# Three reorderings in a Fourier-mixing and MLP kernel: bank copies and gelus, two builds and an output, the queues of the final stores

## The chip, the cores and the metric

The kernel runs on one core of one Trainium2 chip. A core has five engines that work through their own instruction streams and meet at semaphores: TensorE (PE in the profile, its weight loads PEld), VectorE (DVE), ScalarE (ACT), GpSimd (POOL) and SyncE (SP). SP, ScalarE and GpSimd can issue DMAs. TensorE writes its sums into eight banks of PSUM, each 128 partitions by 512 fp32 values.

The metric is the device time of one execution in microseconds. Before the change it is 861.91 us, the median of three runs (861.89 to 861.96).

## The reference

With x of 2048 rows and 640 columns (fp32), the kernel computes a layer norm without parameters, and adds a Fourier mixing of the result and a two-layer MLP of the result to x:

```python
xn = _layernorm(x)                                   # over the 640 columns
a = einsum("bsd,ed->bse", xn, dft_hid_re)            # DFT along the columns
b = einsum("bsd,ed->bse", xn, dft_hid_im)
y = einsum("ts,bse->bte", dft_seq_re, a) - einsum("ts,bse->bte", dft_seq_im, b)   # along the rows
h = gelu(xn @ w1 + b1)                               # 1536 hidden columns
out = x + y + h @ w2 + b2
```

## The kernel before, in words

All products are fp32 products made of three matmuls (`product`, L274, its matmuls at L277, L278 and L279; `hidden`, L289, at L301): each operand is split into a rounded high part and the rest (`split`, L154: ScalarE makes the high part at L160, VectorE the rest at L161), and high by high, high by low and low by high are summed in one bank. The order of all work is written out by hand: what stands first in the code is first on its engine's queue, and an instruction that waits holds whatever stands behind it on the same engine. The rows are worked on in four blocks of 512.

The first stage is the MLP. Blocks 0 and 1 go through it in the plain way: for each of twelve units of 128 hidden columns, `hidden` (TensorE), `gelu` (ScalarE) and `output` (TensorE, five banks). Meanwhile the layer norm of the later blocks runs.

Blocks 2 and 3 go through the first MLP layer together, in six pairs of units, q = 0 to 5, by a scheme with seven instead of eight products for a two by two block. Each pair has three parts on TensorE: `head(q)` (L799), `mid(q)` (L843) and `finish(q)` (L856). A pair uses five banks, called y, d, x2, z2 and w_. `head` computes into y, ScalarE copies y to x2 (`copy_bank`, L796, with its instruction at L797), `head` goes on into d, and ScalarE copies d to SBUF as `fifth` (L804). `mid` adds a product to y, ScalarE copies y to z2, and TensorE goes on with products into x2 and then into z2; after that VectorE adds `fifth` to y and writes the sum of z2 and `fifth` to w_. `finish` adds the last products to z2, y and w_. `head(q + 1)` stands between `mid(q)` and `finish(q)`, and takes over banks that pair q - 1 has used.

`act(q, blk, k)` (L837) is one gelu on ScalarE: it reads a finished bank of pair q for block 2 (blk 0) or block 3 (blk 1) and parks the result in SBUF. In the loop over q (L1080 to L1110) the gelus of the pair behind, p = q - 1, are issued beside the products of pair q. Where p is even, both gelus of block 2 belong to the loop's start; where p is odd, the first of them was issued in `mid(p)`. `sums_w1` (VectorE), `split_w1` (ScalarE, VectorE; its tile is tw) and `load_rq` (SP) prepare the weights of the next pairs, and `between` is what `mid` calls behind its copy to z2. `prep_w` prepares weights of the Fourier stage (ScalarE and VectorE into wst, in the profile wstp; then GpSimd stores them as wit, L394).

After the pairs comes the second MLP layer, one unit after the other: block 2 for n = 0 to 11 into banks 0 to 4 and then block 3 for n = 12 to 23 into banks 5, 6, 7, 3 and 4. At n = 12 block 3 takes two units together: 18 matmuls into banks 5 to 7, and then those into banks 3 and 4, which block 2 has used. `beside_second(n)` (L1135) is what the other engines do behind unit n: `split_h` (the split of two parked gelu results; its tiles are hs and xtt), the weights of later units, `outs(2, ...)` (L864) at n = 11, and the builds. `outs` puts block 2's five banks out: for each, ScalarE adds the bias in the bank (L344), VectorE transposes it into one of two buffers ot (L347), and GpSimd adds it to x (L349), in the order of banks 3, 4, 0, 1, 2; SP stores the result as ys and later starts the loads of raw.

`build(k, what)` (L561) makes operands of the Fourier stage from the rows of the normed input: k is 0 to 7, xr its loaded rows (`load_xr`, SP, L558), and `what` names the parts made: "ab" (tile xab) or "c" (tile xc). Builds 0 to 3 are also stored to DRAM by GpSimd (`formed`, L1125). Builds 4 and 6 are made in two steps, "ab" first and "c" later.

Then comes the Fourier stage, over 500 us of the span, with the same kind of products on halves of the rows; its last steps store the results. `store` (L1236) issues four DMAs, one for each group of 32 partitions, to rows that lie 16 to a partition; each store's pieces in DRAM are as long as the columns stored, 128 bytes for a chunk of 32 columns. The last block's odd chunk (columns 128 to 160 of each group, `yb4`, tile y) is stored just before the end, and the last two chunks of the other block (k = 2 and 3, tile yo, L1674 to L1681) when TensorE has ended or nearly so: chunk 2 needs a transpose and an add, chunk 3 a transpose alone (L1678) of the very last bank. All stores go by SP unless `on_act` gives the last few of the four to ScalarE's queue; the store before them (`out_b`, tile u) goes by ScalarE's queue as a whole.

Of the kernel before, what the change touches and what calls it, by code (L numbers as in the profile page):

```python
# [16 lines left out]
Q = 4  # L17
B = 32
# [8 lines left out]
def kernel(  # L27
# [38 lines left out]
    nc = tc.nc  # L66
# [11 lines left out]
    DQ = D // Q  # L78
# [576 lines left out]
    for tag, size, keys in PLACES:  # L655
        t = whole[tag] = place(tag, (P, size // 4))
# [13 lines left out]
    last = 1  # L670
# [119 lines left out]
    for _ in range(5):  # L790
        y, d, x2, z2, w_ = PB[-1]
# [45 lines left out]
    def act(q, blk, k):  # L837
        y, d, x2, z2, w_ = PB[q]
        src = ((x2, y), (z2, w_))[blk][k]
        u = 2 * q + k  # L840
        nc.scalar.activation(park(q, blk, k), bank(src), AF.Gelu_apprx_tanh, bias=b1c[:, u : u + 1])
# [148 lines left out]
    for g in range(NG):  # L990
        t, i = divmod(g, NF)
# [87 lines left out]
    late_steps = {1: (6, 7), 2: (8, 9), 3: (10, 11), 4: (12, 13)}  # L1079
    for q in range(1, NF // 2):  # L1080
        p = q - 1
        if not p % 2:
            act(p, 0, 0)
        sums_w1(q + 1)
        act(p, 0, 1)

        def between():
            split_w1(q + 1)
            load_rq(q + 2)
            act(p, 1, 0)  # L1090
            act(p, 1, 1)

        mid(q, between)
        if q < NF // 2 - 1:
            head(q + 1)
        else:
            second(2, 0, 0, HU[0, 0])
            split_h(1)
            for u in (2, 3):
                split_w2(u)  # L1100
                raw_w2(u + 4, u - 2)
        for k in late_steps.get(q, ()):
            prep_w(k)
        finish(q)
        if q == 3:
            split_h(0)
        if q == 4:
            prep_w(14)
            for u in range(2, 6):
                raw_w2(u, u - 2)  # L1110
# [24 lines left out]
    def beside_second(n):  # L1135

        if n % 2 and 2 <= (n + 3) // 2 < NF:
            split_h((n + 3) // 2)
        for u in {1: (4, 5), 2: (6,), 3: (7,), 4: (8,), 5: (9,), 6: (10,)}.get(n, ()):
            late_w2(u)  # L1140
        if n == 6:
            load_xo(2)
        if n in (2, 4, 6, 8):
            formed(n // 2 - 1)
            load_xr((2, 3, 4, 6)[n // 2 - 1])
        if n == 9:
            build(4, "ab")
        if n == 11:
            outs(2, (3, 4, 0, 1, 2))
            A["es"].close()  # L1150
            A["raw"] = pool("rawp")
            load_a(0)
        if n == 12:
            build(6, "ab")
        if n == 13:
            load_a(1)
        if n == 14:
            A["xcp", 0] = place("xc01", (P, 2, 2, 7 * P))
            build(4, "c")
        if n == 16:  # L1160
            build(5)
        if n == 17:
            load_xr(7)
            build(6, "c")
        if n == 19:
            build(7, "a")
        if n == 21:
            A["r01"] = place("r01", (P, 2, 2, 2, TB), F32)
            turn(0, 0)
            turn(0, 1)  # L1170
            A["as"] = place("as", (P, 3, 2, 2, TB))
        if n == 22:
            form(0)
            turn(1, 0)
            turn(1, 1)
            form(1)
        if n == 23:
            form(2)
# [54 lines left out]
            for k in names:  # L1233
                nc.sync.dma_start(part_of(t, k), sums[t, k])

    def store(t, src, c0, c1, on_act=0):  # L1236

        for q in range(Q):
            (nc.scalar if q >= Q - on_act else nc.sync).dma_start(
                rows_of(out, t)[:, :, q * DQ + c0 : q * DQ + c1], src[q * B : (q + 1) * B]  # L1240
            )

# [42 lines left out]
    yo = {}  # L1285
# [183 lines left out]
    def hidden_beside(b, n):  # L1469


        ta, tb = blocks[b - 1][1], blocks[b][1]
        last = b == len(blocks) - 1
        x_, y_, z_ = (banks[:, k : k + 2] for k in (X, Y, Z))
        us, vs = bank(US), bank(VS)
        ya = yo[ta]

        def s(which, k):
            return sums[(ta, tb)[which], k]

        def t2(k):
            return lambda: add(s(1, KU[k]), s(1, KV[k]), s(1, KU[k]), ALU.subtract)

        def t3(k):
            return lambda: add(s(0, KU[k]), s(1, KU[k]), s(0, KU[k]), ALU.subtract)

        def t4(k):
            return lambda: add(s(0, KV[k]), s(0, KV[k]), s(1, KU[k]), ALU.subtract)

        def columns(k):  # L1490

            return s(1 if last else 0, ("u1", "u2")[k]).rearrange("p a b -> p (a b)").rearrange("p (n e) -> p n e", n=NB)

        def load_yb(k):
            return lambda: nc.sync.dma_start(columns(k), ys[k][tb])

        def copy(dst, src):
            return lambda: nc.scalar.activation(dst, src, AF.Copy)

        def to(dst, acc, name, then=lambda: None):  # L1500


            def f():
                add_turned(dst, turned(acc, name))
                then()

            return f

        def out_a(c0, c1):
            return lambda: store(ta, ya[:, :, c0:c1], c0, c1) if last else None  # L1510

        def odd():
            yt = turned(us, f"yo_{tb}")
            add_turned(ya[:, :, 4 * B :], yt)
            add_turned(yo[tb, 4], yt)
            out_a(4 * B, DQ)()

        def in_two(k):

            acc, name = s(1, ("v2", "v1")[k]), f"yb{k}_{tb}"  # L1520

            def f():
                if name not in A:
                    A[name] = turned(acc, name)
                else:
                    add_turned(columns(k), A.pop(name))
                    out_b(k)()

            return f

        def out_b(k):
            return lambda: store(tb, columns(k), 2 * k * B, 2 * (k + 1) * B, Q if last and k == 1 else 0)

        def last_columns():

            A["end"] = A["rt2"][:, 0, 0, 0]
            nc.vector.transpose(A["end"].rearrange("p (n i) -> p n i", i=B), ya[:, :, 3 * B : 4 * B])

        yb1, yb2 = in_two(0), in_two(1)
        yb4 = to(yo[tb, 4], vs, f"yb4_{tb}", lambda: store(tb, yo[tb, 4], 4 * B, DQ))  # L1540
        f5s = [lambda u=u: f5(u) for u in range(2)] if not last else [lambda: None] * 2
        f6s = [lambda u=u: f6(u) for u in range(2)] if not last else [lambda: None] * 2
        v1 = lambda: add(s(1, "v1"), s(1, "v1"), x_)
        end = lambda: add(bank(X + 1), bank(X + 1), A["end"])
        pre = [v1] if n == 17 and not last else []
        post = {

            0: [lambda: gather(1, tb, "v1", z_), lambda: gather(1, tb, "v", vs, op=ALU.subtract), f5s[0]],
            1: [f5s[1]],
            3: [to(ya[:, :, : 2 * B], x_, f"ya1_{ta}")],  # L1550
            2: [last_columns] if last else [],
            4: [t2(0)],
            5: [t2(1)],
            6: [to(ya[:, :, : 2 * B], y_, f"ya2_{ta}", out_a(0, 2 * B)), t2(2)],
            7: [odd],
            8: [t3(0)],
            9: [copy(s(1, "v1"), z_), t3(1)],
            10: [t3(2)],
            11: [t4(0)],
            12: [copy(s(1, "v2"), x_), t4(1)],  # L1560
            13: [load_yb(0), t4(2), load_yb(1)] if last else [t4(2)],
            14: [lambda: add(s(1, "v2"), s(1, "v2"), z_), yb1],
            15: [yb1] if last else [load_yb(0)],
            16: [] if last else [load_yb(1)],
            17: [v1, end, yb2, yb2] if last else [yb1, yb2],
            18: [yb4] if last else [yb2],
            19: [f6s[0]],
            20: [] if last else [f6s[1], yb4],
        }.get(n, [])
        if not last:  # L1570
            if n in (12, 13):
                post.insert(0, lambda: load_g(b, (NW - 1) * ND + 13 - n))
            if n == 18:
                post[:0] = [lambda k=k: load_part(blocks[b + 1][1], k) for k in ("u1", "u")]
            if n == 20:
                post.append(lambda: load_a(put_off[0]))

                def end():
                    to(ya[:, :, 2 * B : 4 * B], x_, f"ya3_{ta}")()
                    store(ta, ya, 0, DQ)  # L1580

                later.append(end)
        return pre, post
# [88 lines left out]


    t = blocks[-2][1]  # L1674
    for k, on_act in ((2, Q), (3, Q // 2)):
        d = yo[t][:, :, k * B : (k + 1) * B]
        if k == 3:
            nc.vector.transpose(d, bank(X + 1).rearrange("p (n i) -> p n i", i=B))  # L1678
        else:
            add_turned(d, turned(bank(X), f"yt_{k}"))  # L1680
        store(t, d, k * B, (k + 1) * B, on_act)  # L1681


# [29 lines left out]
```

## Time and profile before

| what | us |
|---|---|
| median of three runs | 861.91 |
| profiled execution, its own time | 858.26 |
| its span, first to last instruction | 856.5 |
| TensorE busy | 843.5 |
| VectorE busy | 661.5 |
| ScalarE busy | 353.7 |
| GpSimd busy | 45.5 |

The profile is one execution, and its time stands 3.65 us below the median of the runs. The granted clock of TensorE was 0.998 over the span. The page of the profile gives busy times and the costliest groups of instructions. The waits list who waited for whom, with the total, the number and the longest. The chain of waits follows the work that ended last back to the start. The timeline lists instructions in order of time: start and duration in us, engine, line, operation, what it writes and reads, the count where several are merged, and in brackets how long its engine had been idle before and what ended that. A `q` behind an engine's name (SPq, ACTq) is its queue of DMA issues. For a DMA, "landing" is the time from its issue to its completion.

### The profile page before, as it was taken

What the parts mean: (1) busy time and instruction counts of PE and PEld (TensorE: products, weight loads), DVE (VectorE), ACT (ScalarE), POOL (GpSimd) and SP (SyncE); (2) the same over time, 40 slices, a digit from 0 to 9 for tenths busy, and PEclk for the clock granted to TensorE, in tenths of its full rate; (3) what the DMA queues carried; (4) which work ended last, traced back from release to release, by engine and by line L of the source; (5) the groups of instructions that cost most, each with busy time, mean ns of one, the idle gap of its engine ahead of it and who ended that gap; (6) DMA issues with size and microseconds to landing.
All of it is one profiled execution on the core that took longest, in us unless ns stands there. A gap on an engine that the chain in (4) does not pass through costs nothing.

```text
span 856.5 us, 10320 instructions
## 1 busy us (share of the span) xinstructions
PE 843.5 (98%) x3711; PEld 695.7 (81%) x3711; DVE 661.5 (77%) x831; ACT 353.7 (41%) x495; POOL 45.5 (5%) x65
## 2 busy tenths in 40 slices
PE   7999999999999999999999999999999999999997
PEld 6888888878878788888888888888888888888885
DVE  6644756786657788889988787998977998885686
ACT  6443634456656544334434334232322423222241
POOL 0000211031211120000000000000000000000000
PEclk9999999999999999999999999999999999999999
DMA  6657698937669998938843769753765779704464
GB/s 185 201 153 200 141 226 240 216 82 189 203 210 341 356 209 156 205 86 199 183 136 86 184 194 302 167 136 98 205 172 168 253 183 233 304 19 178 124 180 96
DMA packets 209219, 158.45 MB, mean 185 GB/s; under 512 B 82896, under 2 KB 182736, under 8 KB 208656
## 3 DMA queue, kind: packets, MB, share of 16 engines
q1 hardware_dynamic: 199936, 136.16, 62.3%
q0 software_dynamic: 3952, 20.71, 6.0%
q10 hardware_dynamic: 5280, 0.92, 0.6%
q8 instruction: 29, 0.48, 0.2%
q14 instruction: 22, 0.18, 0.1%
HBM read 114.76 MB, written 42.99 MB: 184 GB/s over the span
## 4 chain that ended last, share of the span: by engine, by line
PE 84%; issue 7%; DMA 4%; POOL 2%; DVE 2%; ACT 1%; SPq 1%; POOLq 0%; DVEq 0%; ACTq 0%
PE banks L277 25%; PE banks L278 25%; PE banks L279 25%; PE banks L301 10%; DMA xr<-xs 1%; POOL wit L394 1%; DMA wz<-in_A_dft_hid_im_dram 1%; DMA x<-in_A_x_dram 1%; DMA forms_c<-xcst 1%; POOL xo L349 1%; DMA ys<-xo 0%; SPq L364 0%; PE banks L667 0%; DMA rq<-in_B_w_dram 0%; DVE xtt L161 0%
## 5 line engine op out<-in xcount | busy, mean ns | idle before, releaser
L279 PE MATMUL banks<-as,xab 128*128 128x512 f32 x411 | 159.9, 389 | 0.0
L277 PE MATMUL banks<-as,xab 128*128 128x512 f32 x411 | 159.9, 389 | 0.0
L278 PE MATMUL banks<-as,xab 128*128 128x512 f32 x411 | 159.9, 389 | 0.0
L160 ACT ACTIVATE as<-r 128x1024 fp32r<-128x1024 f32 x80 | 85.0, 1062 | 175.8 <-PE banks L279 155.5
L161 DVE TENSOR_TENSOR as<-r,as 128x1024 fp32r<-128x1024 f32 x80 | 97.1, 1215 | 41.7 <-ACT as L160 41.7
L277 PEld LDWEIGHTS banks<-as,xab 128*128 128x128 f32 x411 | 77.1, 188 | 16.1
L278 PEld LDWEIGHTS banks<-as,xab 128*128 128x128 f32 x411 | 77.1, 188 | 16.0
L279 PEld LDWEIGHTS banks<-as,xab 128*128 128x128 f32 x411 | 77.1, 188 | 15.9
L277 PE MATMUL banks<-as,xc 128*128 128x512 f32 x224 | 87.1, 389 | 0.0
L278 PE MATMUL banks<-as,xc 128*128 128x512 f32 x224 | 87.1, 389 | 0.0
L279 PE MATMUL banks<-as,xc 128*128 128x512 f32 x224 | 87.1, 389 | 0.0
L160 ACT ACTIVATE as<-rt 128x1024 fp32r<-128x1024 f32 x32 | 34.0, 1063 | 70.5 <-PE banks L279 62.5
L301 PE MATMUL banks<-xtt,xab 128*128 128x512 f32 x240 | 56.7, 390 | 0.0
L301 PEld LDWEIGHTS banks<-xtt,xab 128*128 128x128 f32 x240 | 44.9, 188 | 9.5 <-DVE xtt L161 0.2
L277 PEld LDWEIGHTS banks<-as,xc 128*128 128x128 f32 x224 | 42.0, 188 | 8.8
L278 PEld LDWEIGHTS banks<-as,xc 128*128 128x128 f32 x224 | 42.0, 188 | 8.7
L279 PEld LDWEIGHTS banks<-as,xc 128*128 128x128 f32 x224 | 42.0, 188 | 8.7
L161 DVE TENSOR_TENSOR as<-rt,as 128x1024 fp32r<-128x1024 f32 x32 | 38.7, 1211 | 5.3 <-ACT as L160 5.3
L320 DVE TENSOR_TENSOR hs<-ab,hs 128x512 fp32r<-128x512 f32 x24 | 17.6, 732 | 32.1 <-ACT hs L318 32.1
L160 ACT ACTIVATE as<-u 128x1024 fp32r<-128x1024 f32 (+1 forms) x24 | 22.1, 919 | 48.2 <-PE banks L279 48.2
L488 DVE STREAM_TRANSPOSE r<-raw 128x1024 f32<-128x1024 f32 x32 | 39.5, 1239 | 0.9 <-PE banks L279 0.3
L488 DVE STREAM_TRANSPOSE rt<-raw 128x1024 f32<-128x1024 f32 x32 | 38.8, 1230 | 0.9 <-PE banks L279 0.8
(335 smaller groups left out, 1615.3 us busy)
## 6 DMA issues: line engine op xcount, KB each, us to landing
raw<-in_A_dft_seq_re_dram SPq DMA_DIRECT2D x64, 256.0 KB, 5.4
raw<-in_A_dft_seq_im_dram SPq DMA_DIRECT2D x64, 256.0 KB, 5.2
ws<-wit SPq DMA_DIRECT2D x15, 384.0 KB, 5.2
x<-in_A_x_dram SPq DMA_DIRECT2D x16, 320.0 KB, 4.6
xs<-x SPq DMA_DIRECT2D x64, 80.0 KB, 1.8
xo<-in_A_x_dram SPq DMA_DIRECT2D x16, 320.0 KB, 6.4
xab<-wit SPq DMA_DIRECT2D x13, 384.0 KB, 4.1
wit<-wstp POOLq DMA_DIRECT2D x12, 384.0 KB, 4.4
```

The source lines that it names most:

```text
L160: nc.scalar.activation(h, s, AF.Copy)
L161: nc.vector.tensor_tensor(l, s, h.bitcast(F32), op=ALU.subtract)
L277: nc.tensor.matmul(acc, wh, mh, start=first, stop=False, skip_group_check=goes_on)
L278: nc.tensor.matmul(acc, wh, ml, start=False, stop=False, skip_group_check=goes_on)
L279: nc.tensor.matmul(acc, wl, mh, start=False, stop=last, skip_group_check=goes_on)
L301: nc.tensor.matmul(acc, W1[i][:, a, j * P : (j + 1) * P], XT[j][:, b], start=n == 0, stop=n == len(steps) - 1)
L320: nc.vector.tensor_tensor(hs[:, 1], a, hs[:, 0].bitcast(F32), op=ALU.subtract)
L349: eng.tensor_tensor(d, d, yt.rearrange("p (n i) -> p n i", i=B), op=ALU.add)
L394: nc.gpsimd.dma_start(wits[w][j], t[:, :, :n].bitcast(F32))
L488: nc.vector.transpose(held(pieces[g][2], u).rearrange("p c (n i) -> p c n i", i=B), r.rearrange("p n (c i) -> p c n i", i=B))
```

## The change

There are three edits.

First, in the loop over the pairs the gelus of block 2 of the pair behind move from ahead of `mid(q)` into `between`, so that on ScalarE they come behind the copy of y to z2 and ahead of `split_w1`. `sums_w1` stays where it was.

Second, "ab" of build 4 moves from n = 9 to n = 12 and "ab" of build 6 from n = 12 to n = 13 in `beside_second`. On ScalarE and VectorE they thereby come behind the split of n = 11 and `outs(2, ...)`, and build 6 behind the split of n = 13.

Third, `store` takes a list of queues. The odd chunk's four stores of the last block go by GpSimd's queue instead of SP's. Chunks 2 and 3 of the end alternate between SP and ScalarE; before, chunk 2 went by ScalarE alone and chunk 3 half by SP, half by ScalarE.

```diff
     for q in range(1, NF // 2):
         p = q - 1
-        if not p % 2:
-            act(p, 0, 0)
         sums_w1(q + 1)
-        act(p, 0, 1)
 
         def between():
+            if not p % 2:
+                act(p, 0, 0)
+            act(p, 0, 1)
             split_w1(q + 1)
             load_rq(q + 2)
             act(p, 1, 0)
...
-        if n == 9:
-            build(4, "ab")
         if n == 11:
             outs(2, (3, 4, 0, 1, 2))
...
         if n == 12:
+            build(4, "ab")
+        if n == 13:
             build(6, "ab")
-        if n == 13:
             load_a(1)
...
-    def store(t, src, c0, c1, on_act=0):
+    def store(t, src, c0, c1, on_act=0, queues=None):
 
         for q in range(Q):
-            (nc.scalar if q >= Q - on_act else nc.sync).dma_start(
+            (queues[q] if queues else nc.scalar if q >= Q - on_act else nc.sync).dma_start(
...
-        yb4 = to(yo[tb, 4], vs, f"yb4_{tb}", lambda: store(tb, yo[tb, 4], 4 * B, DQ))
+        yb4 = to(
+            yo[tb, 4], vs, f"yb4_{tb}", lambda: store(tb, yo[tb, 4], 4 * B, DQ, queues=[nc.gpsimd] * Q if last else None)
+        )
...
-    for k, on_act in ((2, Q), (3, Q // 2)):
+    for k, queues in ((2, [nc.sync, nc.scalar] * 2), (3, [nc.sync, nc.scalar] * 2)):
...
-        store(t, d, k * B, (k + 1) * B, on_act)
+        store(t, d, k * B, (k + 1) * B, queues=queues)
```

## The prediction

> **What bounds the kernel now.** I read the page first, then the waits of TensorE, then the chain of waits, and last the timelines of the engines around each wait of the chain.
>
> ```profile
> span 856.5 us, 10320 instructions
> PE 843.5 (98%) x3711; PEld 695.7 (81%) x3711; DVE 661.5 (77%) x831; ACT 353.7 (41%) x495; POOL 45.5 (5%) x65
> ```
>
> TensorE is busy for 98% of the span, and no edit changes a matmul. Time can only come from its idle places and from what lies behind its last matmul. Its waits are few (columns: total, times, longest, us):
>
> ```profile
> PE banks L667 <- DVE xp L208: 2.4, 1, 2.4
> PE banks L648 <- DVE warm L639: 1.9, 1, 1.9
> PE banks L277 <- DVE ot L347: 1.5, 1, 1.5
> PE banks L277 <- ACT banks L797: 1.0, 1, 1.0
> ```
>
> The first two are the start, which the edits leave alone. The other two, L347 (outs) and L797 (copy_bank), are what the first two edits move. The chain of waits shows the larger one in order of time, and the end (start, duration, what):
>
> ```profile
> 283.06 12.02 DMA xr<-xs
> 295.10 1.14 ACT xab L582 x3
> 296.24 0.96 ACT xtt L160
> 297.22 1.23 DVE xtt L161
> 298.45 0.64 DVE ot L347
> 299.13 0.50 PE banks L277
> 299.63 0.23 PE banks L278
> ...
> 850.04 0.24 PE banks L279
> 850.30 0.72 DVE yo L1678
> ```
>
> A load of 12.02 us holds the fifth build on ScalarE (xab), the split queued behind it follows, then the transpose that frees the bank, then TensorE. In flow a matmul starts 0.23 us after the last one, while its row lasts 0.39 us; a wait counted from the modelled end is therefore 0.16 us short of the time lost. Behind the last matmul (850.28) the span runs another 6.2 us.
>
> ```profile
> 246.36 0.50 PE L277 MATMUL banks<-xtt,tw 128*128 128x512 f32 x1 [1.04 <-ACT banks L797]
> ```
>
> ```profile
> 299.13 0.50 PE L277 MATMUL banks<-hs,xc01w 128*128 128x512 f32 x1 [1.46 <-DVE ot L347]
> ```
>
> **Edit 1: copies ahead of gelus.** Five bank copies pass eight gelus on ScalarE (two where the pair behind is even, one where it is odd). Nothing is added, and no DMA or VectorE instruction moves against its own queue.
>
> ```profile
> 193.89 0.58 ACT L797 ACTIVATE banks<-banks 128x512 f32<-128x512 f32 x1
> 194.38 1.05 ACT L160 ACTIVATE tw<-rq 128x1024 fp32r<-128x1024 f32 x1
> 198.71 0.58 ACT L797 ACTIVATE banks<-banks 128x512 f32<-128x512 f32 x1 [1.54 <-PE banks L279]
> ...
> 244.57 1.25 ACT L841 ACTIVATE pa<-banks,b1c 128x512 f32<-128x512 f32 x2
> 245.71 0.60 ACT L797 ACTIVATE banks<-banks 128x512 f32<-128x512 f32 x1
> 246.22 1.26 ACT L841 ACTIVATE pb<-banks,b1c 128x512 f32<-128x512 f32 x2
> ```
>
> In the last pair the copy starts at 245.71 behind two gelus and TensorE starts when it ends (246.31 + 0.05 = 246.36). In front it starts at 244.57, where the gelus did: 1.14 us earlier. TensorE would then start at 245.22; its last matmul before was 0.39 + 1.04 us ahead of 246.36, at 244.93, and in flow the next is due at 245.16. So 0.06 us of the wait stays and **1.14 us** is gained. The gelus end as before (the pb row still begins at 246.22), so the banks of pair 4 come free as before or, for the first two, 0.5 us later, at 246.35; the first matmul that writes one of them is due after six more matmuls, 245.22 + 1.4 = 246.6.
>
> In the other pairs TensorE does not wait for this copy, so I cost them at nothing, and the cover must be named. In pairs 1 and 3 the copy itself waits for TensorE, and the two gelus now fall between it and the tw split, which goes back by their 1.14 us: from 194.38 to 195.52, its end to 196.6.
>
> ```profile
> 195.47 1.23 DVE L161 TENSOR_TENSOR tw<-rq,tw 128x1024 fp32r<-128x1024 f32 x1 [3.66 <-ACT tw L160]
> 196.61 1.38 DVE L428 TENSOR_TENSOR banks<-banks,fifth 128x512 f32<-128x512 f32 x2
> ```
>
> VectorE then ends tw at 197.87 and the two bank sums at about 199.1. The next head's product with tw begins when its six matmuls before it end (the copy at 198.71 waits for them): 198.45. Cover 0.6 us. finish's product over the second bank begins six matmuls later, 199.81: cover 0.7 us. Both are thin. If they were gone, each microsecond beyond them would be lost at two places; none is, by these rows. Pairs 2 and 4 keep their tw split, which waits for VectorE's sums of weights. Queued behind the split is SP's load of rq, needed a whole pair (12 us) later.
>
> **Edit 2: builds five and seven follow block 2's outputs.** Four ScalarE and five VectorE instructions of build 4 go behind the split of n = 11 and outs, and those of build 6 behind the split of n = 13. No DMA is moved: ys stores and raw loads stay behind outs on SP, and earlier outs lets them go earlier.
>
> ```profile
> 289.80 1.05 ACT L160 ACTIVATE hs<-pb 128x1024 fp32r<-128x1024 f32 x1
> 297.10 2.94 ACT L344 ACTIVATE banks<-banks,b2c 128x512 f32<-128x512 f32 x5
> ```
>
> On the clock of before: the split follows hs on ScalarE at 290.8, done on VectorE (1.23 us, behind hs there) by about 293.4. TensorE lost 1.46 + 0.16 = 1.62 us, so without the wait its matmul would come at 297.51; 18 matmuls stand before it (4.08 us), so block 2's last unit is issued by 293.43. Two biases of 0.59 us (2.94/5) and two transposes of 0.64 us end near 294.9. That is 2.6 us before 297.51, so the wait goes entirely: **1.62 us**. What is late next: VectorE stands in outs for POOL.
>
> ```profile
> 299.21 6.49 POOL L349 TENSOR_TENSOR xo<-xo,ot 128x512 f32<-128x512 f32 x5 [7.63 <-DVE ot L347]
> ```
>
> Five adds at 1.3 us with two buffers hold the last transpose until near 298, and build 4's sums start behind it. Before, build 4 stood for its load until 295.10, and outs behind it waited for the same POOL adds until they neared their end at 305.7, with build 6 behind them. So build 6 and the splits behind it end earlier, not later. I cost that at nothing.
>
> **Edit 3: the end.** The odd chunk's four stores leave SP for GpSimd, and the eight last ones alternate between SP and ScalarE (four each; before two and six).
>
> ```profile
> 849.22 0.95 ACTq L1239 DMA_DIRECT2D out_dram<-yo  x2
> 851.57 1.50 ACTq L1239 DMA_DIRECT2D out_dram<-yo  x3
> ```
>
> ```profile
> 847.67 2.08 SPq L1239 DMA_DIRECT2D out_dram<-y  x4
> 851.05 0.85 SPq L1239 DMA_DIRECT2D out_dram<-yo  x2
> ```
>
> ScalarE issues two, stands from 850.17 to 851.57, then issues four, the last at 853.11:
>
> ```profile
> L1239 ACTq DMA_DIRECT2D out_dram<-yo x1: 499/499/499, 853.1 to 853.1; - x1
> DMA to landing us min/median/max: 2.1/2.1/2.1
> ```
>
> It lands at 855.2, and 1.3 us later the span ends. The stand fits a completion semaphore that the odd chunk's second store held (issued 848.03, lands after 3.5 us):
>
> ```profile
> L1239 SPq DMA_DIRECT2D out_dram<-y x1: 573/573/573, 848.0 to 848.0; - x1
> DMA to landing us min/median/max: 3.5/3.5/3.5
> ```
>
> In the changed program's order the last ScalarE store waits for the first chunk-2 store on SP in this way. That one is issued at 849.22 and lands 2.1 to 3.5 us later (the two rows just shown), 851.3 to 852.7; the last store is then issued at 851.5 to 852.7 and lands at 853.6 to 855.2. Gain 0 to 1.6 us; I take the middle, **0.8 us**, since the rows of three queues still overlap.
>
> GpSimd's price for a store of 512 runs of 128 B isn't in the trace. The nearest rows are its weight stores, of 128 runs (three column groups together) or 256 (two):
>
> ```profile
> L394 POOL DMA_DIRECT2D wit<-wstp x21: 539/558/951, 203.0 to 245.4; - x21
> DMA to landing us min/median/max: 2.4/4.2/5.5
> ```
>
> Flat, four cost 4 x 0.56 = 2.2 us, the last issued at 849.3, landing by 849.3 + 4.2 = 853.5, under the end above. In proportion to runs from the longest row (0.95 us at 256), 1.9 us each: issued to 855.3, landing near 857.7, 2.5 us after 855.2. I take the flat value, as 128 and 256 runs give nearly the same, and keep 2.5 us of loss as the other end.
>
> The rows of the engines at the end (span, then PE, PEld, DVE, ACT, POOL, clock, DMA share, GB/s):
>
> ```profile
> 851.00:852.00 1.00, 0.00 (x0) 0.00 (x0) 0.02 (x1) 0.00 (x0) 0.00 (x0) 1.00 0.81 96
> 853.00:854.00 1.00, 0.00 (x0) 0.00 (x0) 0.00 (x0) 0.00 (x0) 0.00 (x0) 0.55 1.07 166
> ```
>
> They are less loaded while ScalarE stands than after, so an earlier issue has room. [...]
>
> **The sum.** 1.14 + 1.62 + 0.8 = 3.56 us against the profiled execution's own 858.26 (span 856.5): 854.7. The runs shown have a median of 861.91, 3.65 us above it; I take the gain over unchanged: **858.4 us**.
>
> **The rivals.** About 0.2% (1.7 us) is what a measurement of this kernel can tell from no change.
> - *Slower: GpSimd's stores end last.* With t us per store, issued one behind the other from 847.67 and landing 2.4 us after the last, the end is 847.67 + 4t + 2.4. It passes 855.2 at t = 1.3, eats TensorE's gain of 2.76 at t = 2.0, and from t = 2.4 the kernel is slower by over 0.2%; at t = 2.6 the end is 860.5, 5.3 us later than before, and the time 861.91 - 2.76 + 5.3 = 864.4. For it: two to four times the runs of the rows, and a GpSimd that issued nothing for 500 us. Against: 128 and 256 runs at 0.54 to 0.95 us, which puts 512 at 1.9 at most. Chance 0.06. The milder half, t = 1.5 to 2.4, gives 860.0 to 863.6: chance 0.09.
> - *One wait comes back elsewhere.* A cover of 0.6 us fails in pairs 1 and 3, or the transposes wait for something not seen here. Of the 2.76 us some 1.2 to 1.6 stay, with the tail's 0.8 in all 2.0 to 2.4: 859.5 to 859.9. For it: the thin covers. Against: they are the same rows in a new order. Chance 0.10.
> - *The tail gains nothing.* The engines and not the issue set the end: the same bytes have to land, and a landing of 3.5 us beside 2.1 us shows them queueing. 861.91 - 2.76 = 859.2. Chance 0.15.
> - *No change.* The waits of the profiled execution are not in the runs shown, which take 3.65 us longer for a reason the profile can't show: 861.9. Chance 0.05.
>
> **How the numbers follow.** The forecast has 0.55, with its own range 857.6 (tail 1.6) to 858.9 (tail 0.3). The range goes from 857.4 to 860.9, into the milder GpSimd case; outside lie no change, the slower rival and half of the milder one, 0.16. Faster: 0.55 + 0.15 + 0.10 + 0.02 of the milder case = 0.82; same: 0.05 + 0.07 = 0.12; slower 0.06.
>
> **What would show it.** Edit 1: the L797 row gone from TensorE's waits, the pair's copy ahead of pa, tw split of pair 1 about 1.2 us later and no new wait for tw or for bank sums. Edit 2: the L347 row gone, ot transposes beside the last matmuls of block 2, the xr load out of the chain. TensorE's last matmul near 847.5. Edit 3: chunk stores on both queues without the stand of 1.4 us, the last landing some 4.1 instead of 4.9 us after the last matmul, POOL's four rows of about 0.6 us. The prediction is wrong if POOL's rows are over 1.3 us each or land last, or if a new row of over 0.5 us stands among TensorE's waits.

## The result, and the profile after

| | before | changed |
|---|---|---|
| median of 8 runs each, side by side, us | 859.73 (856.63 to 861.96) | 854.82 (853.63 to 855.13) |
| ratio, 95% interval | | 0.9943 (0.9921 to 0.9964) |
| profiled execution: its own time, span | 858.26, 856.5 | 854.27, 852.5 |
| start of the first transposes (L667), us | 11.09 | 9.69 |
| start of the last matmul | 849.88 | 846.07 |
| last landing | 855.21 | 851.18 |

The change is faster by 4.9 us in the medians, where 3.5 us was predicted, and its time is 3.6 us below the predicted 858.4. The kernel before has a median of 859.73 here, not the 861.91 of the three runs that the prediction started from (they are among the eight). A second difference turned out to be the key: the kernel before scatters by 5 us over these runs, the changed one by 1.5.

The page after, first two lines, which answer to those shown of before:

```profile
span 852.5 us, 10322 instructions
PE 844.2 (99%) x3711; PEld 696.2 (82%) x3711; DVE 660.9 (78%) x831; ACT 354.2 (42%) x495; POOL 48.2 (6%) x69
```

TensorE's waits after (total, times, longest, us):

```profile
PE banks L648 <- DVE warm L639: 1.9, 1, 1.9
PE banks L667 <- DVE xp L208: 0.3, 1, 0.3
```

The rows of L347 (1.5) and L797 (1.0) are gone, as edits 1 and 2 were to do. The row of L667 is the start: 2.4 us before, 0.3 here. No edit touches the start; the loads of x simply landed earlier in this execution (the slowest of the first four took 4.3 us to land, 6.0 us before). In the profiles below this row lies between 0.9 and 2.6 us, so the 1.4 us that the first transposes gained is one execution's luck and not the change. Edit 1 on ScalarE, and what TensorE does then (timeline: start, duration):

```profile
243.38 0.58 ACT L797 ACTIVATE banks<-banks 128x512 f32<-128x512 f32 x1
243.89 1.24 ACT L841 ACTIVATE pa<-banks,b1c 128x512 f32<-128x512 f32 x2
245.03 1.26 ACT L841 ACTIVATE pb<-banks,b1c 128x512 f32<-128x512 f32 x2
```

```profile
244.27 0.39 PE L279 MATMUL banks<-xc,as 128*128 128x512 f32 x1
244.50 0.39 PE L277 MATMUL banks<-xtt,tw 128*128 128x512 f32 x1
```

The copy stands ahead of pa, and the matmul that waits for it starts 0.23 us behind the one ahead of it, the pace of flow. Edit 2 (ScalarE's timeline around block 2's outputs):

```profile
290.94 3.08 ACT L344 ACTIVATE banks<-banks,b2c 128x512 f32<-128x512 f32 x5 [0.88 <-PE banks L279]
293.92 1.26 ACT L582 ACTIVATE xab<-xr 128x384 fp32r<-128x384 f32 x3
```

The biases now wait for TensorE (0.88 us), not TensorE for them, and the build follows. The chain of waits has no xr load and no gap there. Edit 3 (one tile's instructions: GpSimd's four rows with the smallest, median and largest duration in ns, and their landing):

```profile
L1238 POOL DMA_DIRECT2D out_dram<-y x4: 648/656/696, 844.2 to 846.1; - x4
DMA to landing us min/median/max: 2.8/3.0/3.6
```

### The profile page after: what moved, and what is told of

It is laid out like the page before. It is cut to its first block, busy times and chain, and to the rows that moved or that the text cites. A ratio compares the mean times of both kernels' runs of the same rounds, so it can differ in the third digit from the quotient of the medians.

```text
span 852.5 us, 10322 instructions
## 1 busy us (share of the span) xinstructions
PE 844.2 (99%) x3711; PEld 696.2 (82%) x3711; DVE 660.9 (78%) x831; ACT 354.2 (42%) x495; POOL 48.2 (6%) x69
## 4 chain that ended last, share of the span: by engine, by line
PE 98%; DMA 0%; DVE 0%; SPq 0%; issue 0%; ACT 0%; DVEq 0%; ACTq 0%
PE banks L277 29%; PE banks L279 29%; PE banks L278 29%; PE banks L301 10%; DMA x<-in_A_x_dram 0%; PE banks L667 0%; DVE st L185 0%; SPq L178 0%; DVE yo L1679 0%; DVE mv L186 0%; DVE xp L208 0%; ACT mv L192 0%; DVE mv L194 0%; DVE mv L195 0%; DVE mv L196 0%
## 5 line engine op out<-in xcount | busy, mean ns | idle before, releaser
L161 DVE TENSOR_TENSOR as<-u,as 128x1024 fp32r<-128x1024 f32 (+1 forms) x24 | 24.9, 1041 | 18.8 <-ACT as L160 18.8
```

The lines of the kernel that those rows point to most:

```text
L161: nc.vector.tensor_tensor(l, s, h.bitcast(F32), op=ALU.subtract)
```

## The experiments

Four kernels ran beside the kernel before on one chip, then four on a second, then four on a third. The kernel before had medians of 859.73, 858.56 and 858.33 us there.

**One edit at a time.** Each kernel is before with the named part of the diff shown above, nothing else: edit 1 alone, edit 2 alone, edit 3 alone, and edits 1 and 2 without 3.

> Edit 1 alone: the gelus of the pair behind move behind the bank copy; builds and stores as before. Theory (each removed wait is worth its own loss): the 1.04 us wait for the copy goes, 1.1 to 1.2 us of time lost before, the 1.46 us wait for the transposes stays, so 1.1 us faster than before. Rival (the last wait swallows it: the transposes behind block 2 hang on loads and stores that do not move with TensorE): the wait for the transposes grows by the same 1.1 us and the time does not change. A new wait of under 0.8 us in pair 2 is set by the weight load there and appears whenever the start was early, with or without this edit; the rival to that is that this edit makes it.

> Edit 2 alone: builds five and seven behind block 2's outputs; gelus and stores as before. Theory: the wait for the transposes goes entirely, 1.6 us faster than before, and the 1.04 us wait for the copy stays. Rival (the time of before changes from run to run with how late the loads behind builds land, up to 5 us): this edit alone takes away most of that scatter and gains 3 us or more in the median. If pair 2 waits here too although the gelus are in their old place, the wait there is not made by edit 1.

> Edit 3 alone: odd chunk's stores on GpSimd, the last two chunks alternating between SP and ScalarE. Theory Q (the issue queues set the end): the last landing comes 0.8 us sooner after the last matmul (4.1 instead of 4.9 us), time 0.8 us faster. Theory E (the 16 engines set the end, the bytes are the same): under 0.3 us, the last two chunks land over 3 us after their issue instead of 2.1 to 2.6. Both of TensorE's waits, 1.46 and 1.04 us, stay.

> Edits 1 and 2 together, stores as before. Theory: both waits go, TensorE ends 2.7 us earlier for the same start, time 2.7 us faster than before; with theory E of the stores this is within 0.3 us of the whole change, with theory Q 0.8 us short of it.

| kernel, 12 runs (before: 35) | median, us | lowest to highest | TensorE waits for ot / for the copy |
|---|---|---|---|
| before | 859.73 | 856.28 to 865.99 | 1.5 / 1.0 (its profile) |
| edit 1 | 859.33 | 856.20 to 865.18 | 1.5 / none |
| edit 2 | 855.84 | 854.66 to 856.74 | none / 0.9 |
| edit 3 | 858.97 | 856.70 to 865.84 | 1.7 / 0.3 |
| edits 1 and 2 | 855.29 | 854.25 to 856.43 | none / 0.2, in pair 0 |

Edit 2 is worth 3.89 us in the medians (2.4 to 5.5 by the 95% interval of the ratio), 2.4 times its term of 1.62. Edit 1 is worth 0.4 us alone, too little to be told from the scatter there, and 0.55 us behind edit 2. Edit 3 alone gains 0.8 us, also inside the scatter; behind the other two some 0.5 us (855.29 to 854.82 and 854.75 on other chips). The wait for the copy is a draw, too: 1.0 us in the profile of before, 0.3 in that of edit 3 alone, where no gelu has moved. The column that stands out is the spread. The kernels without edit 2 spread over 9.0 to 9.7 us, the two with it over 2.1 and 2.2 us. Edit 2's kernel holds a hint in its profile, which shows its xr load and then ScalarE:

```profile
L558 SPq DMA_DIRECT2D xr<-xs x2: 395/496/597, 282.0 to 282.7; - x2
DMA to landing us min/median/max: 16.8/17.0/17.1
```

```profile
292.34 3.08 ACT L344 ACTIVATE banks<-banks,b2c 128x512 f32<-128x512 f32 x5 [1.25 <-PE banks L279]
298.92 0.53 ACT L582 ACTIVATE xab<-xr 128x384 fp32r<-128x384 f32 x1 [3.50 <-DMA xr<-xs]
```

The same load that took 12.02 us in the profile of before took 17.1 us here, and cost nothing: the biases are already behind ScalarE when it stands for the load. It landed at 299.87, 4.8 us later than in the profile of before (283.06 + 12.02 = 295.08); in the order of before the biases and TensorE would have stood that much longer. So the theory was formed: **the wait for ot is the wait for this load, the load's duration varies from one execution to the next, and the profile of before had caught a short one.**

**Is it the load?** Two edits test that from both sides without moving a build. The first lets the load go alone: the two GpSimd stores of build 2 go out four units later. In the profile of before they were under way beside it: issued at 282.65 and 284.91 us, they landed 11.6 and 12.2 us after that, while the load ran from 283.06 to 295.08.

```diff
-        nc.gpsimd.dma_start(forms_ab[k], A["xab", k].bitcast(F32))
-        nc.gpsimd.dma_start(forms_c[k], A["xc", k].bitcast(F32))
+        ... (for k == 2 the same two stores are issued by beside_second at n == 10)
```

> The kernel before, with one thing changed: build 2's two stores to DRAM on GpSimd's queue go out behind n = 10 instead of n = 6, so that the load for build 4 (issued at n = 6) isn't on the DMA engines beside them. No build is moved. Theory L (the wait for ot is the wait for this load, whose duration varies from run to run): the load takes under 11 us instead of 12, the ot row of TensorE's waits falls from 1.5 to 1.7 us to under 0.5, and the time goes to that of the kernel with edit 2 alone, about 856 us, its runs within 2 to 3 us of each other instead of 10. Rival W (the builds' work on ScalarE and VectorE ahead of the outputs costs the time, whenever the load lands): the ot row stays at 1.3 us or more and the time at 859 to 860.

```profile
L558 SPq DMA_DIRECT2D xr<-xs x1: 384/384/384, 282.1 to 282.1; - x1
DMA to landing us min/median/max: 7.1/7.1/7.1
```

The load takes 7.1 us, no row for ot is left among TensorE's waits, the median is 855.54 us (3.0 us below before on that chip), and the runs lie between 854.34 and 857.51. A kernel in which no build moved gains what edit 2 gains. The work of the builds, which is as much as before and in the same place, does not cost the time; the load does, and it took 12.02 us with the two stores beside it (the profile of before) and 7.1 us without them (here).

The second makes the load late, once in the order of before and once in the changed one, by giving its turn to the load of build 6:

```diff
-            load_xr((2, 3, 4, 6)[n // 2 - 1])
+            load_xr((2, 3, 6, 4)[n // 2 - 1])
```

> The kernel before, with the loads for builds 4 and 6 issued in the other order, so that build 4's load is issued about 7 us later and lands near 302 us. Theory L: build 4 at n = 9 holds the outputs until then, so the ot row of TensorE's waits is 6 to 9 us (1.5 before), and the time 5 to 8 us above before: 864 to 868. Rival W: the wait does not follow the load, time within 1 us of before.

> The changed kernel with the same swap of the two loads. Theory L: build 4 stands behind the outputs at n = 12, so a load that lands near 302 us costs at most its last microseconds behind the outputs on ScalarE, none of them on TensorE's path: no row of over 0.3 us for ot, time within 0.7 us of the changed kernel (854.1 to 855.5). Rival: the builds are now what the next stage waits for, and a load that is 7 us later costs 2 us or more there: 857 or more.

TensorE's waits in the order of before:

```profile
PE banks L277 <- DVE ot L347: 9.2, 1, 9.2
```

The time is 867.29 us (865.87 to 868.44), 8.7 us above the median of before on that chip. The same late load in the changed order costs nothing: 854.54 us, and no row for ot. The two kernels are 12.75 us apart, with the same loads, builds and outputs. About 1 us of that belongs to edits 1 and 3, which the second has as well (855.84 with edit 2 alone against 854.82 with all three); the rest is edit 2.

The first of the two went slightly past what was expected (5 to 8 us), and the stretches around the wait say why (span, then PE, PEld, DVE, ACT and POOL busy, the granted clock, DMA share, GB/s):

```profile
299.00:300.00 1.00, 0.00 (x0) 0.00 (x0) 0.58 (x2) 0.52 (x1) 0.00 (x0) 1.00 1.03 430
300.00:301.00 1.00, 0.00 (x0) 0.00 (x0) 0.40 (x1) 0.00 (x0) 0.00 (x0) 0.68 0.63 264
301.00:302.00 1.00, 0.00 (x0) 0.00 (x0) 0.00 (x0) 0.00 (x0) 0.00 (x0) 0.50 0.11 46
...
309.00:310.00 1.00, 1.00 (x4) 0.81 (x3) 0.48 (x1) 0.00 (x0) 1.00 (x2) 0.50 0.00 0
310.00:311.00 1.00, 1.00 (x4) 0.77 (x4) 1.00 (x2) 0.00 (x0) 1.00 (x1) 0.70 0.00 0
311.00:312.00 1.00, 1.00 (x6) 0.78 (x6) 1.00 (x2) 0.47 (x2) 1.00 (x2) 1.00 0.00 0
```

```profile
296.56 0.39 PE L279 MATMUL banks<-hs,xc01w 128*128 128x512 f32 x1
306.14 0.80 PE L277 MATMUL banks<-hs,xc01w 128*128 128x512 f32 x1 [9.20 <-DVE ot L347]
...
309.29 0.63 PE L278 MATMUL banks<-hs,xc01w 128*128 128x512 f32 x1
309.72 0.63 PE L279 MATMUL banks<-hs,xc01w 128*128 128x512 f32 x1
...
311.07 0.39 PE L277 MATMUL banks<-xtt,xc01w 128*128 128x512 f32 x1
```

TensorE's last matmul ends near 296.95. The granted clock goes to 0.50 some 3.4 us later (0.68 over the slice from 300 is 1.00 for its first 0.36 us), and comes back near 310.6 (0.70 over its slice), 4.5 us after TensorE has started again. Matmuls come 0.43 us apart in that time instead of 0.23: 12 of them take 4.93 us (306.14 to 311.07) instead of 12 x 0.228 = 2.73, so the wait of 9.35 us (9.58 less one step of 0.23) costs another 2.2. What sets the 3.4 and the 4.5 us is not shown. The trace of the changed kernel with swapped loads has the low clock behind a shorter wait: TensorE waited for 2.5 us at the start (L667), worked on, and the clock still stood at 0.50 from about 11.98 to 15.40 us (0.99 over the slice from 11, 0.80 over the one from 15).

The spread of before fits this. Its runs each come with a mean granted clock. All 102 of the three chips:

| mean granted clock | runs | time, us | median, us |
|---|---|---|---|
| 0.998 and over | 52 | 856.28 to 859.94 | 857.46 |
| 0.996 and 0.997 | 21 | 858.80 to 862.16 | 860.37 |
| 0.995 | 20 | 861.06 to 865.39 | 863.03 |
| 0.993 and 0.994 | 9 | 864.00 to 866.92 | 865.82 |

The slower a run, the lower its clock, down to the 0.993 that the late load of the swap shows in its profile. In the swap the late load stops TensorE for 9.35 us, the clock falls to 0.50 in that time, and the wait is paid for a second time with 2.2 us. A clock of 0.996 or 0.997 alone is no sign of this wait: 6 of the 103 runs of the nine kernels with edit 2 show it, and in the one profile among them (the changed kernel with swapped loads, 0.996) the fall lies at the start. But 29 of the 102 runs of before have 0.995 or less, and none of those 103. That the slower runs of before had this very wait longer is inferred from the clock and from the experiments that move it; no run of before with a long wait was profiled. One thing doesn't fit smoothly: among the thirteen profiles with the two stores beside it, the second of these loads took 10.7 to 13.4 us in twelve and 17.1 us in one, a smaller share than those 29 runs. Whether profiled executions have fewer long loads, the runs can't tell.

**Where edit 1's gain went.** In pair 5 it brought what was expected. But from mid of pair 1 to mid of pair 3 TensorE takes 24.49 us in the profile of before and 25.24 in that of the changed kernel. VectorE there (start, duration, idle before), the first fence before, the second after:

```profile
201.36 0.85 DVE L372 STREAM_TRANSPOSE wz<-wz 128x640 f32<-128x640 f32 x1 [2.25 <-DMA wz<-in_A_dft_hid_im_dram]
...
206.67 1.60 DVE L428 TENSOR_TENSOR rq<-rq 128x512 f32<-128x512 f32 x3
209.40 1.22 DVE L161 TENSOR_TENSOR tw<-rq,tw 128x1024 fp32r<-128x1024 f32 x1 [1.13 <-ACT tw L160]
210.54 1.29 DVE L428 TENSOR_TENSOR banks<-banks,fifth 128x512 f32<-128x512 f32 x2
```

```profile
200.73 0.84 DVE L372 STREAM_TRANSPOSE wz<-wz 128x640 f32<-128x640 f32 x1 [2.34 <-DMA wz<-in_A_dft_hid_im_dram]
...
206.05 1.60 DVE L428 TENSOR_TENSOR rq<-rq 128x512 f32<-128x512 f32 x3
208.78 1.22 DVE L161 TENSOR_TENSOR tw<-rq,tw 128x1024 fp32r<-128x1024 f32 x1 [1.13 <-ACT tw L160]
209.92 1.29 DVE L428 TENSOR_TENSOR banks<-banks,fifth 128x512 f32<-128x512 f32 x2
```

A load of Fourier weights (wz) starts a row of VectorE work that ends in the sums of weights (rq), the tw split beside pair 2 and, behind it, that pair's two bank sums. Before, the split ended at 210.62 and TensorE loaded its low part in flow at 210.92; the bank sums ended at 211.83 and the first product over one of them began in flow at 212.05. That is 0.2 to 0.3 us of slack at both places. After, all of TensorE is 1.4 us earlier (the start), the load only 0.6, and TensorE's weight loads (PEld) stand at both places:

```profile
210.05 0.19 PEld L279 LDWEIGHTS banks<-r,tw 128*128 128x128 f32 x1 [0.38 <-DVE tw L161]
...
211.26 0.19 PEld L277 LDWEIGHTS banks<-r,tw 128*128 128x128 f32 x1 [0.44 <-DVE banks L428]
```

The early start is not what makes this wait. Edit 3 alone began as early as edit 1 alone (first transposes at 9.92 and 9.90 us), and from mid 1 to mid 3 it took 24.54 us where edit 1 took 25.09; what was expected of edit 1 alone, that an early start brings the wait with or without the edit, did not hold. Counted from the first matmul of pair 1's mid, worked out from the traces of all kernels:

| kernels | 16 KB instruction packet on the DMA engines | last im load of wz lands | mid 1 to mid 3 |
|---|---|---|---|
| 5 without edit 1 | 5.8 to 6.5 us | 8.85 to 9.17 | 24.49 to 24.70 |
| 7 with edit 1 | 6.65 to 7.5 | 9.05 to 9.74 | 24.58 to 25.33 |
| 2 with edit 1 and the sums moved (below) | 6.75, 7.57 | 9.08, 9.65 | 24.48, 24.53 |

Within the middle row the last column goes up with the landing, from 9.05 and 24.58 (odd chunk on SP) over 9.19 and 24.72 (the changed kernel, second profile) to 9.74 and 25.33 (edits 1 and 2). The landing in turn goes with the time at which one 16 KB packet of instructions passes through the engines, in the middle of these loads. With edit 1 it passes 1.0 us later in the mean (7.15 against 6.16). Why edit 1 moves it stays open. It is hardly ScalarE's code: the 29 packets of this queue stand 112 to 151 matmuls of TensorE apart over the whole span of the changed kernel (127 in the mean), with anything from 7 to 37 of ScalarE's instructions between two of them, so by these counts they go with TensorE's stream. That the landing sets the wait can be tested, by taking the sums of weights out of its shadow:

```diff
-        sums_w1(q + 1)
+        if q == 1:
+            sums_w1(2)
...
-        for k in late_steps.get(q, ()):
+        for i, k in enumerate(late_steps.get(q, ())):
...
+            if i == 0:
+                sums_w1(q + 2)
```

> The changed kernel, with VectorE's sums of weights for pair q + 1 moved from the top of the loop to pair q - 1, between its two late weight steps, so that the split of pair q's weights stands earlier on VectorE. Theory P (edit 1 gives back 0.6 to 0.8 us at pair 2, because VectorE ends the split of tw too late there when the load of the weights lands late): from pair 1's mid to pair 3's the matmuls take 24.5 us instead of 25.2, and the time is 0.5 to 0.9 us below the changed kernel, 853.9 to 854.3. Rival: the load of the weights itself sets that wait, or the late weight steps take the place of the sums: 25.2 us again and no change, 854.8, or slower where a later pair's weights come too late.

It took 853.91 us (853.12 to 854.39), 0.63 us less than the changed kernel with swapped loads on the same chip. To have the difference itself, the changed kernel and this one ran again side by side.

> The changed kernel itself, beside the three variants of it on one chip, so that tenths of a microsecond can be compared. 854.3 to 855.0, pair 1's mid to pair 3's 24.8 to 25.3 us, last landing 5.1 to 5.3 us behind the start of the last matmul.

> The variant with the sums of weights between the late weight steps, once more. Theory P: 24.5 us from pair 1's mid to pair 3's, and 0.5 to 0.9 us below the changed kernel of the same chip. Rival: the difference seen before lay between executions, and the two agree within 0.2 us.

854.75 us (853.86 to 855.47) against 853.98 (853.29 to 855.42): 0.77 us, and the rival, that the two agree within 0.2 us, is out. VectorE in the second:

```profile
202.55 1.60 DVE L428 TENSOR_TENSOR rq<-rq 128x512 f32<-128x512 f32 x3
...
207.75 1.23 DVE L161 TENSOR_TENSOR tw<-rq,tw 128x1024 fp32r<-128x1024 f32 x1 [0.35 <-ACT tw L160]
```

The sums come 3.5 us earlier, and mid 1 to mid 3 takes 24.48 us, and 24.53 in the first run although its load landed as late as 9.65 us. The changed kernel's own 24.72 was just below what was expected of it, so pair 2 explains only 0.24 us of the difference. The rest lies from mid 3 to the matmul of mid 5 that waited for the copy in before (28.48 against 27.88 us), where the sums of pair 4 stand in the same place; before had it too, with 29.55 us less its wait of 1.20. This kernel is the fastest one measured.

**Which part of edit 3 works.** Two kernels take back half of it each: the odd chunk's stores on SP's queue (`queues=None`), and chunks 2 and 3 on the queues of before:

```diff
-    for k, queues in ((2, [nc.sync, nc.scalar] * 2), (3, [nc.sync, nc.scalar] * 2)):
+    for k, queues in ((2, [nc.scalar] * Q), (3, [nc.sync] * 2 + [nc.scalar] * 2)):
```

> The changed kernel with the odd chunk's four stores back on SP's queue; chunks 2 and 3 still alternate. Theory E (the sixteen engines set the end, edit 3 gains some 0.3 us by earlier issue of the last stores): the last landing comes 5.2 to 5.5 us behind the start of the last matmul instead of 5.1 to 5.3, and the time is 0 to 0.3 us above the changed kernel. Rival Q (a queue of its own for the odd chunk is what lets the chunks go): over 5.5 us and 0.4 us or more above.

> The changed kernel with chunks 2 and 3 on the queues of before (two stores on SP, six on ScalarE); the odd chunk stays on GpSimd. Theory E: ScalarE's six issues end some 0.5 to 0.9 us later, and the last landing comes 5.4 to 5.7 us behind the start of the last matmul; 0.2 to 0.5 us above the changed kernel. Rival: which queue issues them makes no difference (within 0.1 us), because the engines take the same bytes.

| kernel | median, us | start of the last matmul to last landing, us | last issue behind the last matmul's start |
|---|---|---|---|
| changed (same chip) | 854.75 | 5.23 | 2.46 |
| odd chunk on SP | 854.60 | 5.31 | 2.56 |
| old chunk queues | 855.00 | 5.48 | 3.75 |
| before (profile) | 859.73 | 5.34 | 3.23 |

GpSimd's part is worth nothing that can be measured (0.15 us the other way). The shared chunks are worth some 0.25 us in the medians, which the scatter of these runs (854.22 to 856.56 with the old chunk queues) can't tell from nothing; the way to the last landing is longer by the same 0.25 us. With the old chunk queues the last store is issued 1.29 us later and lands only 0.25 us later: the time from its issue to its landing falls from 2.76 to 1.73 us. Over all profiles, the way from the last matmul to the last landing is 5.34 to 6.08 us in six kernels with the old queues (mean 5.57) and 5.11 to 5.32 in six with edit 3 (mean 5.24): 0.33 us. This is one profile of each kernel. With the new chunk queues the earlier issue thus mostly became a longer way to landing (2.76 against 1.73 us); what sets that way is not shown.

## Why the prediction was wrong

*What bounds the kernel.* Right: TensorE's idle places and the tail were all there was, and the two rows named are the ones that went.

*Edit 1, 1.14 us.* The copy's place, the gelus' and the matmul's new start came out as worked out. In the profiles TensorE's way from mid 3 to the matmul of mid 5 that had waited fell from 29.55 to 28.35 us, 1.20. The step that failed is "In the other pairs TensorE does not wait for this copy, so I cost them at nothing". It looked at pairs 1 and 3, where the cover of 0.6 us held, and set pairs 2 and 4 aside because their tw split waits for VectorE's sums. Behind those sums pair 2 had 0.2 to 0.3 us of slack, at its tw split and at its bank sums, and 0.09 to 0.84 us was given back there (24.58 to 25.33 us against the 24.49 of before; the other kernels without edit 1 had 24.49 to 24.70). In the medians some 0.55 us is left, less than what these runs can tell from nothing with certainty. That is the rival "one wait comes back elsewhere" in kind, at a place it did not name and at half its size.

*Edit 2, 1.62 us.* The mechanism was right: outs finds ScalarE and VectorE free, and the load leaves the chain. The size was not: 3.89 us in the medians. The 1.62 us was read from one execution whose load took 12.02 us, as if that were the load's duration. For runs like that one the term was about right: 14 of the 35 runs of before on that chip have a clock of 0.998 or more, and their median, 857.85, is 2.0 us above edit 2's 855.84. The other 21 have a median of 861.64, 5.8 us above it. What was late next was rightly found to be nothing: builds 4 and 6 have room, even for a load that lands 7 us later.

*Edit 3, 0.8 us.* GpSimd's stores cost 0.65 to 0.70 us each where 0.56 was taken, and both rivals in which they end last are out; the last of them lands at 849.75, well ahead of the end. The last ScalarE store did wait for the first chunk-2 store of SP: that one landed at 848.20 and the store was issued at 848.22 (848.80 and 848.82 in the changed kernel's second profile). But the landing 4.1 us behind the end of the last matmul did not come (4.72, before 4.95), as the earlier stores took 3.0 to 3.4 us from issue to landing where before had 2.1 to 2.9 us for chunk 3. The rival "the tail gains nothing" is nearer: 0.33 us of 0.8 stayed.

*The sum, and where it missed.* Against the profiled execution's own 858.26 it gave 854.7; the changed kernel's median is 854.82. That this fits so well is luck in part, as the terms of edits 1 and 3 were twice what stayed of them: against the 52 runs of before with a clock of 0.998 or more (857.46) the changed kernel gains 2.6 us and not 3.56. Against the median of 861.91 it gave 858.4, which is the forecast, and which is 3.6 us too high. "I take the gain over unchanged" is the step that failed. It took the 3.65 us between the profile and the runs for something outside the kernel's waits that the change would leave alone. The experiments point to the same wait, longer: with edit 2, or with the two stores out of the load's way, the median falls by 3.0 to 3.9 us and most of the scatter goes, and a load made late brings the long times and their low clock back (867.29 us, 0.993 in its profile). Whether it was so in those three runs themselves is not shown, as their clocks are not known. They were a draw as well: the median of the 102 later runs of before is 858.99, close to the profiled execution. The rival of no change turned the same gap into the opposite case, that the waits might be absent from the runs; the scatter speaks for longer ones. Once the load is off the path, what the runs had above the profile goes with it.

## What to carry over

When a wait on the critical path ends with a DMA, its size in the profile is one draw: the load here took from 10.7 to 17.1 us in thirteen profiles. If the runs lie above the profiled execution, or scatter, ask first whether that wait is longer in them, and price taking it away by the runs and not by the row. Look also at the granted clock behind a long wait: behind the one of 9.4 us here it was 0.50 for another 4.5 us, which cost 2.2 us more. And slack is to be worked out at each place that waits for the same engine, also at the places that the edit does not seem to touch: here 0.2 to 0.3 us of slack in pair 2 decided over half of edit 1.

## What was not expected of the hardware

- A load of normed rows (xr) with two GpSimd stores beside it landed 10.7 to 17.1 us after its issue in thirteen profiles; without the stores, 7.1 us in one. Why it took 12.0 us in one execution and 17.1 us in another stays open.
- After a wait of 9.4 us the granted clock was 0.50 for another 4.5 us of matmuls, 2.2 us of extra time. After a wait of 2.5 us at the start it was 0.50 for 3.4 us in one profile (the changed kernel with swapped loads), and after one of 2.6 us it did not fall in another (edits 1 and 2, 0.999 over the span).
- One 16 KB packet of instructions, one of 29 that stand 112 to 151 matmuls of TensorE apart, goes with a stretch of some 1.9 us in which none of the im loads of wz land (198.74 to 200.61 in the changed kernel, 198.69 to 200.64 before).
